# Moving the solve, the joining, the masked product and a Gram between the slots of a delta-rule and gated-MLP kernel

## The chip, the cores and the metric

The kernel runs on one core of one Trainium2 chip. The metric is the device time of one execution in microseconds. The kernel before was timed in three runs: the median is 658.25 us, the runs lie between 656.36 and 658.97 us. The profiled execution is a fourth one; its own time is 657.43 us, and its span, from the first to the last instruction, is 655.6 us.

## The reference

A delta-rule recurrence over 768 tokens for 32 heads of width 48 (4 batches of 8 heads), then a gated MLP on the 3072 rows of width 384:

```python
k_n = k / (norm(k) + 1e-06)
for t in range(768):
    y[t] = q[t] @ state
    state = state + beta[t] * outer(k_n[t], v[t] - k_n[t] @ state)
x = y.transpose(0, 2, 1, 3).reshape(3072, 384)
out = (1 / (1 + exp(-(x @ w_gate))) * (x @ w_val)) @ w_out      # 384 -> 1536 -> 384
```

## The kernel before

The tokens are cut into 12 groups of 64 per head, numbered 0 to 11. For each group the 32 heads' recurrence inside the group is solved in closed form, and the group's 256 rows of the MLP follow.

The recurrence of a group g goes through these functions:

- `gram(g)` (L291): 64 small products of K with itself into two PSUM tiles `pg`; then ten copies to SBUF, six into `G` (L303) and four into `L` (L308), on ACT for every group but the first.
- `norms(g)` (L240 to L273): 18 DVE steps that give the norms `m`, `mq` and the factors `gam`.
- `scale_v(g)` (L279): sixteen ACT instructions that scale V in `kv` by `mq`, in place.
- `solve_halves(g)` for groups 0 to 2 (from group 3 on another routine, `solve`, does the work): 40 steps. The first 4 (L382, L385) prepare `H` and `gs`, the next 30 (L391, L394) are the forward substitution, 2 (L397) copy to `X`. Steps 37 to 40 are what is called the joining here: step 37 transposes `X` to `mt` on DVE (L400) and issues the products `pz` (L407, 64 pairs of 32x32 blocks, listed as x128); step 38 transposes `mt` on DVE (L420) and copies `pz` to `scratch` on ACT (L421); step 39 issues the products `pm`; step 40 subtracts `pm` from `mt` (L428, DVE).
- `masked(g)` (L319): the products `pp` of K and Q, then four DVE multiplications by the mask `pmask` (L324) into `kqp`.
- `rest(g)` (L444, L455): products `pk` of K and the state, and R = V - pk on DVE. `updates(g, 0..2)` (L475, L467) use `mt` and R; `rows(g)` (L501, L504) gives Y in `yy`, copied to `ys` (L508, L510); `flip` (L540, L543) transposes it to `xx`, the MLP's input; `advance(g)` (L522) moves the state on.

The MLP's weights come as 36 pieces of 384 KB (`raw`). `scaled(n)` is a pair of ACT instructions on a piece (L189, L191) and also issues the load of piece n + 6; `join(n)` (L203, DVE) makes the words `u` of it; for the groups from 1 on each piece is split further by `weight_hi` (L212, ACT) and `weight_lo` (L219, DVE) into `w`.

The MLP runs in slots. Slot 2f of group 0 issues the products `gv` of the gate and the value for column tile f (L556; L559 from group 1 on), the odd slots the products `po` of the output for the tile two before (L584; L590). Group g's first slot is 24 g. The element-wise work of a tile is the sigmoid on ACT (L564, `sg`) and the product with the value on DVE (L565). What else goes into a slot stands in tables: `plan[s]` is called behind the slot's products, `late[s]` behind its sigmoid, `tail[s]` at the end. Group 1's recurrence runs in the slots of group 0, group 2's in those of groups 0 and 1.

The order in which the code calls is the order of the instructions on each engine, since the schedule is written out by hand for all engines and each engine takes its instructions in that order. The loads are all issued by SP, in code order too: a load that waits holds up those behind it. Buffers are few: `gv` has two PSUM tiles, `aux` (used by `pg`, `pp`, `pz`, `pm`, `pu`, `yy`, `pt`) two, `row` (used by R and by the output rows `ot`) three, `kqp` two and `X`, `G`, `mt` one.

What stands ahead of slot 0 is written out in full: loads, group 0's recurrence up to its `flip`, and pieces of group 1's. `busy_array` there issues products whose result nobody reads. `W` is 24, `plan`'s entries of group 1's solve are in this line, which gives a slot and a number of steps:

```python
    for at, n in ((0, 12), (1, 4), (2, 4), (3, 4), (5, 1), (6, 1), (7, 1), (8, 1)):
        plan[at].append(steps(halves1, n))
```

Of the kernel before, what the change touches and what calls it, by code (L numbers as in the profile page):

```python
# [55 lines left out]
def deltanet_gated_mlp(ctx: ExitStack, tc: tile.TileContext, kd, qd, kv, beta, words, out):  # L56
# [106 lines left out]
    pieces = [(0, "g"), (0, "v")]  # L163
# [112 lines left out]
    def scale_v(g):  # L276
        V, mq = state[g]["kv"][:, 1], state[g]["mq"]
        for c in range(CP):
            nc.scalar.activation(V[:, c], V[:, c], AF.Copy, scale=mq[:, c, 0:1])  # L279
            yield  # L280

    def gram(g):

        kq, st = kqp[g % 2], state[g]
        st["G"] = G = wk.tile([128, 32, CP], F32, name=f"G_{g}", tag="G", bufs=1)
        st["L"] = L = wk.tile([128, CP, 32], F32, name=f"L_{g}", tag="L", bufs=2)
        pg = [ps_aux.tile([128, J, C], F32, name=f"pg_{g}_{e}", tag="aux") for e in range(2)]
        for j in range(J):
            for e, x in KINDS:
                r, t = 64 * e, tokens_at(e, x)  # L290
                nc.tensor.matmul(out=pg[e][t:t + 64, j], lhsT=kq[r:r + D, x, j], rhs=kq[r:r + D, x, j], start=True, stop=True)  # L291
        return blocks_of(pg, G, L, g == 0)
# [332 lines left out]
    def take(gen, n=1):  # L625
        for _ in range(n):
            next(gen, None)
# [32 lines left out]
        pass  # L660
    second_half(half)
    lower_left(0)
    take(scale_v(0), CP)
    take(gram(1), 10)
    halves0, norms1, halves1 = solve_halves(0), norms(1), solve_halves(1)
    for n in range(2, 4):
        scaled(n)
    take(halves0, 38)
    for n in range(4, 8):
        scaled(n)  # L670
    take(norms1, 11)
    take(halves0, 2)
# [5 lines left out]
    busy_array(gap[0], 5)  # L678
    stage(12, 14, lower_left(1))
    load_rows(1, 0)  # L680
    for n in range(8, 10):
        scaled(n)
    take(masks0, 2)
    updates(0, 1)
# [1 line left out]
    take(norms1, NORMS)  # L686
    updates(0, 2)
    busy_array(gap[0], 5)
    for n in range(10, 12):
        scaled(n)  # L690
    take(joins, 2)
    take(halves1, 12)
    rows(0)
    busy_array(gap[0], 2)
    scaled(12)
    take(joins, 2)
    flip(0, 0)
    flip(0, 1)
    busy_array(gap[0], 2)
    tail = collections.defaultdict(list)  # L700
    for n in range(13, len(pieces)):
        plan[(n - 13) * 4 // 5].append(lambda n=n: scaled(n))
    plan[2].append(lambda: load_k(2))
    spread(joins, len(pieces) - 4, 0, 20)
    for at, n in ((0, 12), (1, 4), (2, 4), (3, 4), (5, 1), (6, 1), (7, 1), (8, 1)):
        plan[at].append(steps(halves1, n))
    spread(splits, 12, 7, 24, into=tail)
    spread(splits, len(pieces) + 1 - 12, 24, 44, into=tail)
    for s in (4, 5):
        plan[s].append(steps(scalings[1], 8))  # L710
    for part in (1, 0):
        plan[8].append(lambda part=part: load_rows(2, part))
    plan[10].append(lambda: load_q(2))
    halves2 = solve_halves(2)
    plan[11].append(lambda: clear(2))
    plan[23].append(lambda: joint(2))
    plan[24].append(lambda: lower_left(2))

# [19 lines left out]
    for g in range(N):  # L738
        w = W * (g - 1)
        if g == 0:  # L740
            late[3].append(lambda: advance(0))
            continue
        up, at_rows = (13, 19) if g < 3 else (10, 16)
        late[w + 10 if g == 1 else w + 6].append(lambda g=g: rest(g))
        for step in range(3):
            late[w + up + 2 * step].append(lambda g=g, step=step: updates(g, step))
        late[w + at_rows].append(lambda g=g: rows(g))
        late[w + at_rows].append(lambda g=g: advance(g))
        for c in range(2):
# [93 lines left out]
```

## Time and profile before

| | |
|---|---|
| time of the profiled execution, its span | 657.43 us, 655.6 us |
| median of three runs | 658.25 us (656.36 to 658.97) |
| PE busy | 626.6 us, 96% of the span |
| PE weight loads busy | 585.8 us, 89% |
| DVE, ACT, POOL busy | 467.9 us (71%), 320.9 us (49%), 11.3 us (2%) |
| mean granted TensorE clock | 0.985 |
| the chain that ended last | PE 90%, DVE 4%, ACT 3%, issue 1%, DMA 1% |

The profile's timeline gives, for an engine, the start and the length of an instruction (or of a run of alike ones, x their number), the line, what is written from what, and in brackets the idle time before it with the engine and line that ended it. The lengths of PE's products overlap by some 0.1 us with the next one's start. The windows give the busy time of each engine in a stretch of the span, and the granted clock of TensorE as a share of full speed.

### The profile page before, as it was taken

The numbers are of one execution on the slowest core, as the hardware profiler recorded it, in microseconds if no ns is written. First come the engines' busy times: TensorE is split into PE (matmuls) and PEld (weight loads), VectorE is DVE, ScalarE is ACT, GpSimd is POOL, SyncE is SP. The second block draws the span as 40 slices with busy tenths as digits, with TensorE's granted clock in tenths as the row PEclk, the third lists the DMA queues.
The fourth block names the chain that finished last, engine by engine and source line by source line (L and its number), as shares of the span: only waits on it lengthen the run. The fifth ranks groups of instructions, "written<-read, shape, count | busy, mean of one in ns | idle before, by whom it ended". The sixth has DMA issues, their size and how long they took to land.

```text
span 655.6 us, 24068 instructions
## 1 busy us (share of the span) xinstructions
PE 626.6 (96%) x10548; PEld 585.8 (89%) x10556; DVE 467.9 (71%) x1443; ACT 320.9 (49%) x870; POOL 11.3 (2%) x30
## 2 busy tenths in 40 slices
PE   6776999899999999999999999999999999999996
PEld 4454778798999999999999999999999999999996
DVE  5886398668887877877977967977977977952221
ACT  4957586455554454454454454454354354333321
POOL 5000000000000000000000000000000000000000
PEclk9988899899999999999999999999999999999999
DMA  9586553110222021122012012013012100000101
GB/s 263 184 272 194 166 138 83 26 27 2 83 51 60 26 51 52 38 48 62 29 44 72 23 41 77 22 39 81 21 33 82 23 8 3 19 9 2 25 1 25
DMA packets 17769, 41.07 MB, mean 63 GB/s; under 512 B 4224, under 2 KB 7296, under 8 KB 17664
## 3 DMA queue, kind: packets, MB, share of 16 engines
q1 hardware_dynamic: 17664, 39.53, 21.1%
q8 instruction: 83, 1.36, 0.9%
q14 instruction: 22, 0.18, 0.1%
HBM read 34.80 MB, written 4.72 MB: 60 GB/s over the span
## 4 chain that ended last, share of the span: by engine, by line
PE 90%; DVE 4%; ACT 3%; issue 1%; DMA 1%; ACTq 0%; SPq 0%; DVEq 0%
PE gv L559 43%; PE po L590 22%; PE gv L556 5%; PE pu L475 3%; PE po L584 2%; PE pg L291 2%; PE pk L444 2%; PE yy L501 2%; PE yy L504 2%; PE pp L319 2%; PE pk L467 1%; PE pd L522 1%; PE pt L540 1%; ACT kv L279 1%; DVE kqp L324 1%
## 5 line engine op out<-in xcount | busy, mean ns | idle before, releaser
L559 PE MATMUL gv<-xx,w 128*128 128x256 f32 x2376 | 308.2, 284 | 0.0
L559 PEld LDWEIGHTS gv<-xx,w 128*128 128x128 f32 x2376 | 302.2, 191 | 0.7
L590 PE MATMUL po<-w,h 128*128 128x384 f32 x792 | 166.4, 345 | 0.2 <-issue 0.2
L564 ACT ACTIVATE sg<-gv 128x256 f32<-128x256 f32 x144 | 55.2, 384 | 208.3 <-PE gv L559 193.2
L590 PEld LDWEIGHTS po<-w,h 128*128 128x128 f32 x792 | 133.3, 188 | 3.5 <-issue 0.4
L565 DVE TENSOR_TENSOR sg<-sg,gv 128x256 f32<-128x256 f32 x144 | 60.3, 419 | 90.6 <-ACT sg L564 90.2
L570 ACT CAST h<-sg 128x256 fp32r<-128x256 f32 x132 | 53.6, 406 | 53.1 <-DVE sg L565 51.5
L350 DVE TENSOR_TENSOR X<-X,tmp 128x126 f32<-128x126 f32 (+22 forms) x279 | 71.3, 256 | 8.9
L347 DVE TENSOR_TENSOR tmp<-X,gp 128x126 f32<-128x126 f32 (+22 forms) x279 | 70.9, 254 | 7.9
L575 DVE TENSOR_TENSOR h<-sg,h 128x256 fp32r<-128x256 f32 x132 | 55.0, 417 | 28.1 <-ACT h L570 28.0
L481 ACT COPY su<-pu 32x384 f32<-32x384 f32 x92 | 43.3, 470 | 14.3 <-PE pu L475 12.9
L279 ACT ACTIVATE kv<-kv,mq 128x48 f32<-128x48 f32 x192 | 48.1, 330 | 0.0
L529 DVE TENSOR_TENSOR su<-su,pd 48x384 f32<-48x384 f32 x40 | 22.1, 552 | 20.5 <-PE pd L522 20.1
L556 PE MATMUL gv<-xx,u 128*128 128x256 f32 x144 | 36.4, 405 | 0.0
L303 ACT COPY G<-pg 32x256 f32<-32x256 f32 (+1 forms) x69 | 25.3, 367 | 18.6 <-PE pg L291 17.3
L324 DVE TENSOR_TENSOR kqp<-pp,pmask 64x512 f32<-64x512 f32 x48 | 32.3, 687 | 2.1 <-PE pp L319 1.1
L556 PEld LDWEIGHTS gv<-xx,u 128*128 128x128 f32 x144 | 28.3, 203 | 5.5 <-issue 0.8
L455 DVE TENSOR_TENSOR R<-kv,pk 128x384 f32<-128x384 f32 x44 | 22.4, 550 | 2.1 <-PE pk L444 2.1
L212 ACT CAST w<-u 128x384 fp32r<-128x384 f32 x36 | 18.2, 509 | 5.4 <-DVE w L219 4.9
L475 PEld LDWEIGHTS pu<-R,mt 32*32 32x32 f32 x1408 | 16.5, 105 | 4.9 <-issue 1.2
L475 PE MATMUL pu<-R,mt 32*32 32x48 f32 x1408 | 19.4, 202 | 0.9 <-DVE kqp L324 0.9
L219 DVE TENSOR_TENSOR w<-u,w 128x384 fp32r<-128x384 f32 x36 | 19.3, 551 | 1.3 <-ACT w L212 1.3
(104 smaller groups left out, 517.7 us busy)
## 6 DMA issues: line engine op xcount, KB each, us to landing
raw<-in_words_dram SPq DMA_DIRECT2D x36, 384.0 KB, 5.2
kv<-in_kv_dram SPq DMA_DIRECT2D x24, 384.0 KB, 5.4
kqp<-in_qd_dram SPq DMA_DIRECT2D x24, 256.0 KB, 4.1
kqp<-in_kd_dram SPq DMA_DIRECT2D x24, 192.0 KB, 3.6
out_dram<-ot SPq DMA_DIRECT2D x48, 96.0 KB, 2.2
beta<-in_beta_dram SPq DMA_DIRECT2D x12, 16.0 KB, 4.5
```

What stands on the lines that cost most here:

```text
L279: nc.scalar.activation(V[:, c], V[:, c], AF.Copy, scale=mq[:, c, 0:1])
L347: nc.vector.tensor_tensor(out=tmp, in0=X[:, k:16, j:j + 1].to_broadcast([128, n, j]), in1=gp[:, j:j + 1, 0:j].to_broadcast([128, n, j]), o ...
L350: nc.vector.tensor_tensor(out=X[:, k:16, 0:j], in0=X[:, k:16, 0:j], in1=tmp, op=ALU.add)
L475: nc.tensor.matmul(out=pu[0 if g else x][r:r + 32, j], lhsT=mt[r:r + 32, e * J + j], rhs=R[e][r:r + 32, j], start=True, stop=True)
L481: nc.scalar.copy(su[r:r + 32, 3 if x else e], pu[0][r:r + 32])
L556: nc.tensor.matmul(out=pg[:, o], lhsT=parts[w, f][:, k * 128:(k + 1) * 128], rhs=x[0][:, k], start=k == 0, stop=k == KC - 1)
L559: nc.tensor.matmul(out=pg[:, o], lhsT=parts[w, f][:, a, k * 128:(k + 1) * 128], rhs=x[b][:, k], start=(k == 0 and q == 0), stop=(k == KC - ...
L564: nc.scalar.activation(h, st["gv", f][:, 0], AF.Sigmoid)
L565: nc.vector.tensor_tensor(out=h, in0=h, in1=st["gv", f][:, 1], op=ALU.mult)
L570: nc.scalar.copy(hh[:, 0], st["sg", f])
L575: nc.vector.tensor_tensor(out=hh[:, 1], in0=st["sg", f], in1=hh[:, 0].bitcast(F32), op=ALU.subtract)
L590: nc.tensor.matmul(out=po[s], lhsT=hh[:, a, ts], rhs=parts["o", f][:, w], start=(f == 0 and q == 0), stop=(f == NF - 1 and q == 2))
```

## The change

The ordering in front of slot 0 and the tables of the slots are changed; no instruction is added or removed.

- Ahead of slot 0, G's ten copies of group 1 are issued ahead of group 0's scalings of V, four `scaled` follow ACT's copy of `pz` where two stood ahead of it, and 4 steps of group 1's solve stand ahead of Y's copy, not 12. K of group 2 is loaded there, not in slot 2.
- Group 1's solve: slots 0 to 5 instead of 0 to 3. Its joining: steps 37 to 40 in slots 9, 10, 10, 11 instead of 5, 6, 7, 8.
- Group 1's masked product: slot 11 instead of 1. Its scalings of V: slots 7 and 8 instead of 4 and 5. Its `rest`: slot 8 instead of 10.
- Group 2's Gram: behind slot 3 instead of slot 8, its copies in slots 4 to 6; its norms and solve from slot 8 on instead of 12. Its scalings: slots 25 to 28 instead of 21 to 24; its `rest`: slot 28 instead of 30; its joining: slots 29, 30, 30, 31 instead of 27 to 30.
- `scaled`, the splits and group 2's loads are moved by a slot or two.

```diff
     lower_left(0)
+    take(gram(1), 10)
     take(scale_v(0), CP)
-    take(gram(1), 10)
...
-    for n in range(2, 4):
-        scaled(n)
     take(halves0, 38)
-    for n in range(4, 8):
+    for n in range(2, 6):
         scaled(n)
...
     load_rows(1, 0)
+    load_k(2)
-    for n in range(8, 10):
+    for n in range(6, 9):
         scaled(n)
...
     take(joins, 2)
-    take(halves1, 12)
+    take(halves1, 4)
     rows(0)
...
-    for at, n in ((0, 12), (1, 4), (2, 4), (3, 4), (5, 1), (6, 1), (7, 1), (8, 1)):
+    for at, n in ((0, 8), (1, 4), (2, 6), (3, 4), (4, 5), (5, 5), (9, 1), (10, 1), (11, 1)):
         plan[at].append(steps(halves1, n))
-    spread(splits, 12, 7, 24, into=tail)
+    plan[10].append(steps(halves1))
+    spread(splits, 12, 9, 24, into=tail)
...
-    for s in (4, 5):
+    for s in (7, 8):
         plan[s].append(steps(scalings[1], 8))
...
-        late[w + 10 if g == 1 else w + 6].append(lambda g=g: rest(g))
+        at_rest = {1: 8, 2: 28}.get(g, w + 6)
+        late[at_rest].append(lambda g=g: rest(g))
...
-            mask_later(1, 1)
+            mask_later(1, 11)
...
-            gram_later(g, w - 16 if g < 4 else w - 18)
+            gram_later(g, {2: 3, 3: 32}.get(g, w - 18))
...
-            scaling(g, w - 3 if g == 2 else w - 5 if g == 3 else w - 7)
-    spread(chain(norms(2), halves2), NORMS + 36, 12, 26, lambda s: max(0.1, 1.6 - busy[s]))
-    for at in (27, 28, 29, 30):
+            scaling(g, {2: 25, 3: 43}.get(g, w - 7))
+    spread(chain(norms(2), halves2), NORMS + 36, 8, 27, lambda s: max(0.1, 1.6 - busy[s]))
+    for at in (29, 30, 30, 31):
         plan[at].append(steps(halves2))
```

Three places of the order. The first is DVE ahead of slot 0, from the last preparation of group 1's solve to the copy of Y (`ys`); before:

```order
L385 SCALAR_TENSOR_TENSOR gs_728<-gp_471,gam_668 128x256
L391 TENSOR_TENSOR tmp_15_733<-H_727,gs_728 128x30
L394 TENSOR_TENSOR H_727<-H_727,tmp_15_733 128x2x15
L391 TENSOR_TENSOR tmp_14_736<-H_727,gs_728 128x28
L394 TENSOR_TENSOR H_727<-H_727,tmp_14_736 128x2x14
L391 TENSOR_TENSOR tmp_13_739<-H_727,gs_728 128x52
L394 TENSOR_TENSOR H_727<-H_727,tmp_13_739 128x2x2x13
L391 TENSOR_TENSOR tmp_12_742<-H_727,gs_728 128x48
L394 TENSOR_TENSOR H_727<-H_727,tmp_12_742 128x2x2x12
L508 COPY ys_779<-yy_1_746 128x8x48
```

Now:

```order
L382 TENSOR_TENSOR H_725<-dmask,gam_666 128x128
L385 SCALAR_TENSOR_TENSOR gs_726<-gp_467,gam_666 128x256
L508 COPY ys_765<-yy_1_732 128x8x48
L203 SCALAR_TENSOR_TENSOR u_778<-raw_102 128x384
L203 SCALAR_TENSOR_TENSOR u_778<-raw_106 128x384
```

The eight substitution steps now stand behind `xx`, in slot 0.

The second is DVE ahead of group 1's joining (L400), from the element-wise product of one tile earlier on; before (tile 2, slots 4 and 5):

```order
L565 TENSOR_TENSOR sg_2_992<-sg_2_992,gv_2_966 128x256
L203 SCALAR_TENSOR_TENSOR u_1003<-raw_611 128x384
L203 SCALAR_TENSOR_TENSOR u_1003<-raw_613 128x384
L400 STREAM_TRANSPOSE mt<-X_563 128x16x16x2
L203 SCALAR_TENSOR_TENSOR u_1092<-raw_618 128x384
```

Now (tile 4, slots 8 and 9; `gp_1062` is group 2's norms):

```order
L240 STREAM_TRANSPOSE gp_1062<-G_918 128x1024
L565 TENSOR_TENSOR sg_4_1064<-sg_4_1064,gv_4_1040 128x256
L455 TENSOR_TENSOR R_0_1101<-kv_113,pk_0_1067 128x384
L455 TENSOR_TENSOR R_1_1102<-kv_113,pk_1_1068 128x384
L203 SCALAR_TENSOR_TENSOR u_1111<-raw_776 128x384
L203 SCALAR_TENSOR_TENSOR u_1111<-raw_803 128x384
L400 STREAM_TRANSPOSE mt<-X_559 128x16x16x2
```

R's two subtractions now stand between the tile's product and L400; on ACT the sixteen scalings of V still stand close ahead of that tile's sigmoid.

The third is ACT around group 2's joining, from tile 1's sigmoid of group 1 on (`ot` are group 0's last output rows); before:

```order
L564 ACTIVATE sg_1_1874<-gv_1_1852 128x256
L212 CAST w_1878<-u_1092 128x384
L212 CAST w_1881<-u_1092 128x384
L594 COPY ot_0_1885<-po_0_995 128x384
L594 COPY ot_1_1889<-po_1_996 128x384
L570 CAST h_1_1960<-sg_1_1874 128x256
L212 CAST w_1963<-u_1106 128x384
L421 COPY scratch_1755<-pz_1894 128x512
```

Now:

```order
L564 ACTIVATE sg_1_1866<-gv_1_1839 128x256
L212 CAST w_1870<-u_1013 128x384
L212 CAST w_1873<-u_1013 128x384
L594 COPY ot_0_1877<-po_0_983 128x384
L594 COPY ot_1_1881<-po_1_984 128x384
L279 ACTIVATE kv_1015<-kv_1015,mq_1425 128x48 x4
L570 CAST h_1_1889<-sg_1_1866 128x256
L212 CAST w_1892<-u_1030 128x384
L279 ACTIVATE kv_1015<-kv_1015,mq_1425 128x48 x4
L564 ACTIVATE sg_2_1918<-gv_2_1894 128x256
```

Eight of group 2's scalings of V and tile 2's sigmoid now stand ahead of the joining's copy L421. On DVE, group 2's L400 stood behind tile 1's product and two L219; now it stands behind tile 1's product, three L219, L575, tile 2's product, R's two subtractions and one more L219.

More of the change, by code (lines that the diff above doesn't have):

```diff
@@ L688, in deltanet_gated_mlp @@
     busy_array(gap[0], 5)
-    for n in range(10, 12):
+    for n in range(9, 11):
         scaled(n)
     take(joins, 2)
-    take(halves1, 12)
+    take(halves1, 4)
     rows(0)
     busy_array(gap[0], 2)
-    scaled(12)
+    for n in range(11, 13):
+        scaled(n)
     take(joins, 2)
@@ L700, in deltanet_gated_mlp @@
     tail = collections.defaultdict(list)
-    for n in range(13, len(pieces)):
-        plan[(n - 13) * 4 // 5].append(lambda n=n: scaled(n))
-    plan[2].append(lambda: load_k(2))
+    for n, at in enumerate((0, 0, 0, 1, 2, 2, 4, 5, 6, 8, 9, 10, 11, 12, 12, 13, 14, 15, 16, 16, 17, 18, 18), 13):
+        plan[at].append(lambda n=n: scaled(n))
     spread(joins, len(pieces) - 4, 0, 20)
-    for at, n in ((0, 12), (1, 4), (2, 4), (3, 4), (5, 1), (6, 1), (7, 1), (8, 1)):
+    for at, n in ((0, 8), (1, 4), (2, 6), (3, 4), (4, 5), (5, 5), (9, 1), (10, 1), (11, 1)):
         plan[at].append(steps(halves1, n))
-    spread(splits, 12, 7, 24, into=tail)
+    plan[10].append(steps(halves1))
+    spread(splits, 12, 9, 24, into=tail)
     spread(splits, len(pieces) + 1 - 12, 24, 44, into=tail)
-    for s in (4, 5):
+    for s in (7, 8):
         plan[s].append(steps(scalings[1], 8))
     for part in (1, 0):
-        plan[8].append(lambda part=part: load_rows(2, part))
-    plan[10].append(lambda: load_q(2))
+        plan[6].append(lambda part=part: load_rows(2, part))
+    plan[8].append(lambda: load_q(2))
     halves2 = solve_halves(2)
-    plan[11].append(lambda: clear(2))
+    plan[12].append(lambda: clear(2))
     plan[23].append(lambda: joint(2))
@@ L751, in deltanet_gated_mlp @@
             busy[w + at_rows + 2] += 0.6
-        busy[w + 10 if g == 1 else w + 6] += 1.1
+        busy[at_rest] += 1.1
         busy[w + up + 2] += 1.1
```

## The prediction

> **What bounds the kernel now.** I read the page, then PE's list of waits over the first 130 us, then PE's timeline there with the windows of the granted clock beside it. The chain that ended last is nine tenths PE (the table in front), so what counts is where PE waits and where its clock is low.
>
> ```profile
> PE pz L407 <- DVE mt L400: 6.6, 2, 4.5
> ```
>
> Of PE's waits this is the longest: two joinings wait 6.6 us for DVE's transposition L400. On the timeline the first lies inside group 0's slots, the second where group 1's begin:
>
> ```profile
> 42.63 1.51 PE L540 MATMUL pt<-ident,ys 128*128 128x128 f32 x6 [2.32 <-DVE ys L508]
> 44.88 3.25 PE L556 MATMUL gv<-xx,u 128*128 128x256 f32 x12
> 61.41 1.82 PE L407 MATMUL pz<-mt,scratch 32*32 32x32 f32 x119 [4.46 <-DVE mt L400]
> 65.25 0.33 PE L407 MATMUL pz<-mt,scratch 32*32 32x32 f32 x9 [2.03 <-issue]
> 65.51 4.87 PE L556 MATMUL gv<-xx,u 128*128 128x256 f32 x12
> 70.22 1.45 PE L584 MATMUL po<-u,sg 128*128 128x384 f32 x4
> 71.61 1.29 PE L407 MATMUL pm<-scratch 32*32 32x32 f32 x128
> 72.82 2.86 PE L556 MATMUL gv<-xx,u 128*128 128x256 f32 x12
> 75.61 1.16 PE L291 MATMUL pg<-kqp 48*64 48x64 f32 x64
> 80.78 1.15 PE L444 MATMUL pk<-su,kqp 48*64 48x48 f32 x64
> 108.89 0.82 PE L540 MATMUL pt<-ident,ys 128*128 128x128 f32 x6
> 120.31 1.45 PE L584 MATMUL po<-u,sg 128*128 128x384 f32 x4
> 123.95 1.78 PE L407 MATMUL pz<-mt,scratch 32*32 32x32 f32 x128 [2.19 <-DVE mt L400]
> 125.67 3.29 PE L559 MATMUL gv<-xx,w 128*128 128x256 f32 x18
> 128.80 1.22 PE L590 MATMUL po<-w,h 128*128 128x384 f32 x6
> 131.32 2.42 PE L559 MATMUL gv<-xx,w 128*128 128x256 f32 x18
> ```
>
> ```profile
> 59.00:60.00 1.00, 0.00 (x0) 0.00 (x0) 0.72 (x2) 1.00 (x3) 0.00 (x0) 0.69 0.68 252
> 69.00:70.00 1.00, 1.00 (x4) 0.78 (x3) 0.00 (x0) 0.00 (x0) 0.00 (x0) 0.69 0.00 0
> 124.00:125.00 1.00, 1.00 (x91) 1.00 (x95) 1.00 (x3) 0.79 (x3) 0.00 (x0) 0.62 0.16 35
> ```
>
> A wait costs more than its idle time. The third number from the end is the granted clock: it falls in the window from 59 us and rises in the one from 69, and a gv product between takes 4.87 us, not 2.86. Group 1's joining so loses 4.46 idle, 2.03 of "issue" (PE waits for nothing that the profile shows; its own code, I think), 0.9 in pz (1.82 + 0.33 against pm's 1.29) and 2.0 in gv: 9.4 us. Group 2's loses 2.19, then 0.5 in pz and 0.9 in gv (3.29 against 2.42): 3.6 us. Behind the 2.32 us that Y's transposition waited, gv shows 0.4 too much.
>
> **Ahead of slot 0.**
>
> ```profile
> 23.79 2.06 PE L416 MATMUL pz<-mt,wide 64*64 64x32 f32 x64 [0.28 <-DVE mt L400]
> 26.60 0.58 ACT L421 COPY scratch<-pz 128x512 f32<-128x512 f32 x1
> 38.64 1.14 PE L504 MATMUL yy<-su,kqp 128*64 128x48 f32 x32
> 40.05 0.19 DVE L391 TENSOR_TENSOR tmp<-H,gs 128x30 f32<-128x30 f32 x1
> 41.93 0.56 DVE L508 COPY ys<-yy 128x384 f32<-128x384 f32 x1
> ```
>
> Group 0's pz ended at 25.85, ACT copied it at 26.60, behind two pieces. These now come later, and G's copies and V's scalings take the same time in either order, so L421 starts 0.65 earlier, and with it all that hangs on pm. It is worth 0 if something else holds that chain, 0.75 at most; I take 0.6. Y's products ended at 39.78, but DVE went through eight solve steps from 40.05 to 41.93 before it copied Y: 1.9 us gone, with certainty, as the four steps that stay end at 40.05. The transposition then comes right behind the products, so the clock has no reason to fall, and 1.51 becomes 0.82: 0.65. Sum 3.1 (from 1.9 to 3.3), and 0.4 in slot 0's gv.
>
> The eight steps are now in slot 0, where DVE waited for the sigmoid later on; they cost nothing as long as joins and products of slots 0 to 6 keep ahead of PE, and by my count DVE still idles there before tile 3's product. ACT's three pieces of slot 0 must have landed. K of group 2, 384 KB in two loads, now goes ahead of nine pieces on SP's queue and delays their landing by about a microsecond; a piece is used six pieces after it was asked for, some 6 us, so I take 0. POOL's clearing of X and group 2's other loads move by two slots at most, with nobody near to wait for them.
>
> **Group 1's joining.** Its prices:
>
> ```profile
> 20.87 2.31 ACT L303 COPY G<-pg 128x256 f32<-128x256 f32 x6
> 23.20 1.49 ACT L308 COPY L<-pg 32x256 f32<-32x256 f32 x4
> 53.21 1.92 ACT L527 COPY su<-pd 48x384 f32<-48x384 f32 x4
> 56.93 1.91 ACT L279 ACTIVATE kv<-kv,mq 128x48 f32<-128x48 f32 x8
> 58.86 0.38 ACT L564 ACTIVATE sg<-gv 128x256 f32<-128x256 f32 x1
> 60.02 1.90 ACT L279 ACTIVATE kv<-kv,mq 128x48 f32<-128x48 f32 x8
> 60.55 0.71 DVE L400 STREAM_TRANSPOSE mt<-X 128x512 f32<-128x512 f32 x1
> 81.98 1.02 DVE L455 TENSOR_TENSOR R<-kv,pk 128x384 f32<-128x384 f32 x2 [0.26 <-PE pk L444]
> ```
>
> Before, L400 came late since tile 2's product waited for a sigmoid that stood behind eight scalings (56.93, then 58.86). The new order repeats it at tile 4. I count from the end of the state's product pd in slot 3. PE (overlaps of 0.1 taken off): pg 1.1, three gv of 2.7, two po of 1.4, to the end of tile 4's gv 12.0; then pk 1.1 and po 1.4, so it is ready for pz at 14.5. ACT from the same point: the state's copies 1.9, four pieces of 0.9 (58.86 to 60.02 is a sigmoid of 0.3 and a piece), G's copies 2.3, L's 1.5, two sigmoids 0.6, sixteen scalings 3.8: 13.7, so tile 4's sigmoid, whose gv was done at 12.0, ends at 14.1. DVE then: the product 0.35, R 0.95, two joins 0.95, L400 0.7: 17.0. PE starts pz 0.1 later and has idled 2.6 us (the ends: none, and the 4.46 of before); all of PE's work stands behind pz, so this counts in full. Half clock after that: pz and gv lost 1.4 behind an idle time of 2.19, so I take 1.2, since 2.6 us needn't fall into one window. New loss 3.8 instead of 9.4.
>
> [...]
>
> The new neighbours: pd and pg, 128 small products, now follow each other, where code could come late; between 0 and the 2.03 shown, I take 0.4, as 64 alone showed none at 75.61. The masked product at slot 11 needs pm's buffer, freed by L428. DVE reaches the end of L428 (priced as L400) some 2.4 us after tile 5's gv, PE comes there after pm and po, 2.6 us: nothing, but without spare. Its four masks, 2.7 us on DVE, then lie beside gv of slot 12, before updates in slot 13 that want the buffer. Group 1's `rest` is off the path: mt is needed in slot 13 only.
>
> **Group 2's joining.**
>
> ```profile
> 112.62 1.00 ACT L279 ACTIVATE kv<-kv,mq 128x48 f32<-128x48 f32 x4
> 119.95 1.38 DVE L324 TENSOR_TENSOR kqp<-pp,pmask 64x512 f32<-64x512 f32 x2
> 122.81 0.51 ACT L212 CAST w<-u 128x384 fp32r<-128x384 f32 x1 [1.51 <-DVE w L219]
> 123.22 0.85 ACT L594 COPY ot<-po 128x384 f32<-128x384 f32 x2
> ```
>
> It moves back by one tile, so PE has a gv (2.3), pk (1.1) and a po (1.1) more: on the times of before it would be ready at 121.76 + 4.5 = 126.25, not 121.76 (120.31 + 1.45). But the masks keep DVE busy until 121.33 as before, X's second copy follows them, and the cast that waited until 122.81 waits until 123.0. Behind it ACT has now: casts 0.8, `ot` 0.75, h 0.3, eight scalings 2.0, tile 2's sigmoid 0.4: 127.25. DVE: product 0.35, R 0.95, a split 0.5, L400 0.7, so pz starts at 129.85: idle 3.6 us instead of 2.2 (ends 2.2 and 4.5). With 1.4 for the clock as before this joining loses 5.0, not 3.6: 1.4 worse.
>
> **Sum**, against the profiled execution: -3.1 - 0.4 - 5.6 (9.4 to 3.8) + 0.4 + 1.4 = -7.3, so 657.43 becomes 650.1. The median of the runs shown is 0.8 higher; for runs I say 650.5.
>
> **The rivals.**
> - Group 1's joining is covered after all. For it: ACT's chain has twenty terms, and some copies may run beside gaps that I didn't see; against it: tile 4's sigmoid would have to come 1.5 us sooner and the rest shrink too. It takes away the 3.8: 646.7.
> - Group 1's joining again stops for code (2.03) and pays a second half-clock window (1.7, half of the 3.3 us that the fall at 124 lasted): +3.7, 654.2; with all of before's loss 656. For it: both stood behind each other before. Against: no other pz stopped for code.
> - Y comes no earlier, since something other than the solve steps holds the transposition: +3.1, 653.6. Only the end of yy at 39.78 could, and it allows the gain.
> - Slower: K's load waits for Y's products, as they read the same tile, and holds up the pieces behind it on SP.
>
> ```profile
> 35.26 15.49 SPq L172 DMA_DIRECT2D raw<-in_words_dram  x9
> 86.76 0.84 SPq L105 DMA_DIRECT2D kqp<-in_kd_dram  x2
> 103.69 1.35 SPq L109 DMA_DIRECT2D kqp<-in_qd_dram  x2
> ```
>
> These nine pieces would then start near 40 us, not at 35.26; ACT, which ends ahead of the first joining without idle time, passes each late microsecond on, with half of one more for the clock: 5 us late cost 7.5, and from there on the change loses: 658 to 660. Against it: group 3's K was loaded at 86.76, long before Y's products of group 1, for which its Q waited until 103.69. So K waits for its own readers only.
>
> **How the numbers follow.** 0.5% (3.3 us) is about what a measurement of this kernel can tell from no change, so faster means under 655.0. Forecast 0.55 (648 to 653), covered joining 0.17, code and clock again 0.15 (two thirds of it above 655), no gain at Y 0.08, slower 0.05. Faster: 0.55 + 0.17 + 0.08 and a little of the third; slower 0.05 with its tail; the rest is the same. The range leaves out the slower case, half of the case with code and a part of the covered one: 646 to 656.
>
> **What would show it.** Right: Y's transposition near 40.1 without a wait, slot 0 near 41.8; group 1's pz behind po of slot 9 with 2 to 3 us idle, the sigmoid before it late behind L279; group 2's pz idle 3 to 4 us, longer than before; the rest of the trace alike, shifted. Wrong: idle before pz of group 1 under 1 us or over 4, PE waiting for L428 at the masked product, ACT waiting for pieces in slots 0 to 4, or a stop of PE for code at pd and pg.

## The result and the profile after

The changed kernel took 651.71 us (median of five runs, 650.23 to 653.05), the kernel before 656.36 us in five runs on the same chip (655.90 to 658.97). The ratio is 0.9915, with a 95% interval from 0.9887 to 0.9944: 4.65 us faster, 1.2 us above the 650.5 us that were predicted. The profiled execution took 652.21 us, its span is 650.5 us (before 657.43 and 655.6), and the mean granted clock 0.991 (before 0.985). Of the kernels run later, two executions lie far off and are left out of the figures below: one of 2078.95 us, with the filling products, and one of 687.92 us at a granted clock of 0.844, with the early transpositions and the old slots.

PE's timeline of the changed kernel, at the same places as before: ahead of slot 0, the two joinings, and the updates of groups 1 and 2 (the columns: start, length, engine, line, operation, number, and the idle time ahead with what ended it):

```profile
30.91 0.28 PE L475 MATMUL pu<-kv,mt 32*32 32x48 f32 x5 [1.04 <-issue]
36.83 0.37 PE L475 MATMUL pu<-kv,mt 32*32 32x48 f32 x14 [1.22 <-issue]
41.29 0.84 PE L540 MATMUL pt<-ident,ys 128*128 128x128 f32 x6 [0.44 <-ACT raw L191]
42.88 5.42 PE L556 MATMUL gv<-xx,u 128*128 128x256 f32 x24 [0.31 <-DVE xx L543]
48.22 0.94 PE L522 MATMUL pd<-su,kv 64*48 64x48 f32 x64
48.98 1.13 PE L291 MATMUL pg<-kqp 48*64 48x64 f32 x64
66.53 1.93 PE L407 MATMUL pz<-mt,scratch 32*32 32x32 f32 x128 [3.31 <-DVE n L244]
68.39 5.00 PE L556 MATMUL gv<-xx,u 128*128 128x256 f32 x12
76.02 1.16 PE L319 MATMUL pp<-kqp 48*64 48x64 f32 x64
81.19 0.88 PE L475 MATMUL pu<-R,mt 32*32 32x48 f32 x64
123.58 1.75 PE L407 MATMUL pz<-mt,scratch 32*32 32x32 f32 x128 [3.36 <-DVE mt L400]
125.26 3.34 PE L559 MATMUL gv<-xx,w 128*128 128x256 f32 x18
144.43 0.88 PE L475 MATMUL pu<-R,mt 32*32 32x48 f32 x64 [0.88 <-DVE kqp L324]
```

The same two updates in the kernel before:

```profile
87.23 0.88 PE L475 MATMUL pu<-R,mt 32*32 32x48 f32 x64
149.44 0.88 PE L475 MATMUL pu<-R,mt 32*32 32x48 f32 x64 [0.88 <-DVE kqp L324]
```

Y's transposition waits 0.44 us, not 2.32 (for `ys`, which DVE wrote until 41.14 us), and slot 0 starts at 42.88 us, 2.0 earlier than before. Group 1's joining waits 3.31 us, without the stop of 2.03 us. The name in the bracket, L244, is the instruction that happened to end last by the profile; what pz reads is `mt`, which L400 wrote from 65.68 to 66.39 us. Group 2's joining waits longer than before, 3.36 us against 2.19. Group 1's first update in slot 13 (the pu at 81.19) stood at 87.23 us before, group 2's (144.43) at 149.44: of the 6.04 us won up to the one, 5.01 are left at the other, and 5.1 at the end of the span.

ACT and DVE ahead of group 1's joining:

```profile
58.58 1.90 ACT L279 ACTIVATE kv<-kv,mq 128x48 f32<-128x48 f32 x8
61.28 1.90 ACT L279 ACTIVATE kv<-kv,mq 128x48 f32<-128x48 f32 x8
63.08 0.36 ACT L564 ACTIVATE sg<-gv 128x256 f32<-128x256 f32 x1
60.46 1.24 DVE L240 STREAM_TRANSPOSE gp<-G 128x1024 f32<-128x1024 f32 x1
63.48 0.42 DVE L565 TENSOR_TENSOR sg<-sg,gv 128x256 f32<-128x256 f32 x1 [1.78 <-ACT sg L564]
65.68 0.71 DVE L400 STREAM_TRANSPOSE mt<-X 128x512 f32<-128x512 f32 x1
```

The chain is the one foretold: tile 4's sigmoid ends at 63.44 us behind sixteen scalings, and DVE's product, R, two joins and L400 stand behind it.

Windows of one microsecond of the changed kernel (behind the stretch: its length, then the busy share and instructions of PE, PE's loads, DVE, ACT and POOL, the granted clock, the DMA share, GB/s):

```profile
65.00:66.00 1.00, 0.00 (x0) 0.00 (x0) 1.00 (x3) 0.63 (x2) 0.00 (x0) 0.96 1.07 208
72.00:73.00 1.00, 1.00 (x4) 0.83 (x3) 0.00 (x0) 0.00 (x0) 0.00 (x0) 0.62 0.08 16
123.00:124.00 1.00, 0.42 (x48) 0.46 (x52) 1.00 (x3) 0.10 (x1) 0.00 (x0) 0.98 0.12 21
127.00:128.00 1.00, 1.00 (x9) 1.00 (x9) 0.00 (x0) 0.00 (x0) 0.00 (x0) 0.82 0.00 0
```

Between the rows at 65 and 72, and between those at 123 and 127, the clock is 0.50. So behind two waits of nearly the same length it stayed at half for different times: some 6.8 us from the end of the window at 65 to inside that at 72, and 3.4 us from the end of that at 123 to inside that at 127.

The moments themselves show more. With 1.00 up to the change and 0.50 behind it, a share of 0.96 at 65 puts the fall at 65.92 us, 0.62 at 72 the rise at 72.76, and 0.98 and 0.82 put the second pair at 123.96 and 127.36. Group 1's pz started at 66.53 us, 0.61 behind the fall, and the clock stayed down for 6.8 us; group 2's had started at 123.58, ahead of the fall, and it was 3.4 us. Worked out in the same way from windows of one microsecond of this trace and of those of before and of three kernels below (us):

| kernel | wait | idle | PE back at | clock falls at | time at half clock |
|---|---|---|---|---|---|
| before | Y's transposition | 2.32 | 42.63 | 42.32 | 3.4 |
| before | group 1's joining | 4.46, then the stop of 2.03 inside pz | 61.41 | 59.38 | 10.2 |
| before | group 2's joining | 2.19 | 123.95 | 124.24 | 3.4 |
| changed | group 1's joining | 3.31 | 66.53 | 65.92 | 6.8 |
| changed | group 2's joining | 3.36 | 123.58 | 123.96 | 3.4 |
| four solve steps alone | group 1's joining | 4.95 | 58.77 | 59.06 | 3.4 |
| group 2's joining back | group 1's joining | 5.11 | 67.36 | 65.66 | 6.8 |
| group 2's joining back | group 2's joining | 2.19 | 118.19 | 120.26 | 3.4 |
| masked product moved | group 1's joining | 1.91 | 55.91 | 56.54 | 3.4 |

4.95 us of idle time were followed by 3.4 us at half clock, 3.31 us by 6.8. So the length of a wait alone doesn't set its price.

### The profile page after: what moved, and what is told of

It reads as the page before. It is cut to its first block, busy times and chain, and to the rows that moved or that the text cites. A ratio compares the mean times of both kernels' runs of the same rounds, so it can differ in the third digit from the quotient of the medians.

```text
span 650.5 us, 24072 instructions
## 1 busy us (share of the span) xinstructions
PE 626.4 (96%) x10556; PEld 585.0 (90%) x10556; DVE 467.9 (72%) x1443; ACT 321.2 (49%) x870; POOL 11.3 (2%) x30
## 3 DMA queue, kind: packets, MB, share of 16 engines
q8 instruction: 83, 1.36, 0.9%
## 4 chain that ended last, share of the span: by engine, by line
PE 89%; DVE 5%; ACT 3%; issue 1%; DMA 1%; ACTq 0%; SPq 0%; DVEq 0%
PE gv L559 43%; PE po L590 22%; PE gv L556 4%; PE pu L475 3%; PE pg L291 2%; PE yy L501 2%; PE yy L504 2%; PE pp L319 2%; PE po L584 2%; PE pd L522 2%; PE pk L444 1%; PE pk L467 1%; PE pt L540 1%; ACT kv L279 1%; DVE kqp L324 1%
## 5 line engine op out<-in xcount | busy, mean ns | idle before, releaser
L575 DVE TENSOR_TENSOR h<-sg,h 128x256 fp32r<-128x256 f32 x132 | 55.1, 417 | 29.8 <-ACT h L570 29.8
L556 PE MATMUL gv<-xx,u 128*128 128x256 f32 x144 | 35.8, 402 | 0.3 <-DVE xx L543 0.3
L556 PEld LDWEIGHTS gv<-xx,u 128*128 128x128 f32 x144 | 28.2, 201 | 5.5 <-ACT xx L543 0.8
L475 PEld LDWEIGHTS pu<-R,mt 32*32 32x32 f32 x1408 | 16.5, 105 | 4.9 <-issue 1.7
L219 DVE TENSOR_TENSOR w<-u,w 128x384 fp32r<-128x384 f32 x36 | 19.4, 550 | 1.5 <-ACT w L212 1.4
L475 PE MATMUL pu<-R,mt 32*32 32x48 f32 x1408 | 19.4, 202 | 0.9 <-DVE kqp L324 0.9
```

The lines of the kernel that those rows point to most:

```text
L475: nc.tensor.matmul(out=pu[0 if g else x][r:r + 32, j], lhsT=mt[r:r + 32, e * J + j], rhs=R[e][r:r + 32, j], start=True, stop=True)
L556: nc.tensor.matmul(out=pg[:, o], lhsT=parts[w, f][:, k * 128:(k + 1) * 128], rhs=x[0][:, k], start=k == 0, stop=k == KC - 1)
L575: nc.vector.tensor_tensor(out=hh[:, 1], in0=st["sg", f], in1=hh[:, 0].bitcast(F32), op=ALU.subtract)
```

## The experiments

Eleven kernels were timed in four groups, each in five rounds against the kernel before (medians of before: 656.99, 655.61, 656.08 and 656.07 us). The traces are one execution of each kernel. Ratios are to the kernel before. In the kernels with early transpositions four or five lines are added, so that L400 reads L401, L407 L411, L475 L480, L556 L561 and so on; in the one with filling products two, so that L556 reads L558.

**Which part brings the gain? Four solve steps ahead of Y, alone** (the kernel before, and nothing else of the change):

```diff
-    take(halves1, 12)
+    take(halves1, 4)
...
-    for at, n in ((0, 12), (1, 4), (2, 4), (3, 4), (5, 1), (6, 1), (7, 1), (8, 1)):
+    for at, n in ((0, 20), (1, 4), (2, 4), (3, 4), (5, 1), (6, 1), (7, 1), (8, 1)):
```

> The kernel before with one part of the change: 4 solve steps ahead of Y's copy, the other 8 in slot 0, all else as before. Theory (the steps held Y's copy, and PE's idle time behind it brought the clock down): the transposition starts 1.9 us sooner, takes 0.8 us, not 1.5, gv of slot 0 is 0.4 shorter: slot 0 starts 2.5 us sooner; group 1's joining stays as late against slot 0 as it was or up to 1 us worse, so 1.5 to 3 us less than before. Rival (the gain is given back at the joining, as DVE has 1.9 us more to do ahead of it): the wait at group 1's joining grows from 4.5 to 6.4 us, time as before.

652.48 us (651.26 to 657.39), ratio 0.9939 (0.9912 to 0.9967): the interval overlaps that of the whole change. PE's timeline of this kernel:

```profile
42.16 2.83 PE L556 MATMUL gv<-xx,u 128*128 128x256 f32 x12 [0.31 <-DVE xx L543]
58.77 1.78 PE L407 MATMUL pz<-mt,scratch 32*32 32x32 f32 x128 [4.95 <-DVE mt L400]
81.14 0.88 PE L475 MATMUL pu<-R,mt 32*32 32x48 f32 x64
```

Slot 0 starts 2.7 us earlier than before, about the 1.9 + 0.65 that I had put on Y. Group 1's joining still waits 4.95 us, but the stop of 2.03 us inside it is gone, although nothing was moved there on PE. The first update in slot 13 starts at 81.14 us, and in the changed kernel at 81.19: up to there the four steps alone win as much in these traces as the whole change, with the joining in its old slots.

**G's copies ahead of V's scalings, alone** (the kernel before, with `gram(1)`'s ten copies first and the pieces ahead of slot 0 nearly as in the change):

```diff
     lower_left(0)
+    take(gram(1), 10)
     take(scale_v(0), CP)
-    take(gram(1), 10)
...
-    for n in range(2, 4):
-        scaled(n)
     take(halves0, 38)
-    for n in range(4, 8):
+    for n in range(2, 6):
         scaled(n)
...
-    for n in range(8, 10):
+    for n in range(6, 9):
         scaled(n)
...
-    for n in range(10, 12):
+    for n in range(9, 12):
         scaled(n)
```

> The kernel before with G's copies ahead of V's scalings alone (and its pieces in the order that this gives); Y still behind twelve solve steps, everything else in its old slot. L421 starts 0.7 us earlier. In the kernels run so far PE's stop at the first small products of pu ended at 30.6 to 31.6 us in whichever order ACT works, though PE reached them 0.4 to 0.7 us earlier with G's copies first. If that stop takes the gain, slot 0 starts at 44.5 to 45.2 us (44.88 before) and the time is within 1 us of the kernel before. If the 0.6 us that I predicted come through, slot 0 starts at 44.2 to 44.3, and the time is 1 us lower or more, since the first joining follows.

657.97 us (654.20 to 660.59), ratio 1.0024 (0.9996 to 1.0051): no gain. PE ahead of slot 0, with both of PE's stops, and in group 1's joining:

```profile
30.85 0.28 PE L475 MATMUL pu<-kv,mt 32*32 32x48 f32 x5 [1.31 <-issue]
37.05 0.37 PE L475 MATMUL pu<-kv,mt 32*32 32x48 f32 x14 [1.49 <-issue]
45.63 4.73 PE L556 MATMUL gv<-xx,u 128*128 128x256 f32 x12
67.16 0.33 PE L407 MATMUL pz<-mt,scratch 32*32 32x32 f32 x9 [1.73 <-issue]
```

The last five products of pu's first burst start at 30.85 us; in the kernel before, with a stop of 0.75 us ahead of them, they did at 30.92. PE gets there 0.6 us earlier and stops nearly that much longer. Slot 0 is 0.75 us later than before, since the second stop is longer too (1.49 us, not 0.67).

The stop inside group 1's pz is here again, 1.73 us ahead of the same nine products. So the two traces with twelve solve steps ahead of Y have it, and none of the eleven with four does. That speaks against an accident of one execution; what ties it to those kernels isn't shown.

**Are those stops due to transfers that share the DMA engines?** Two pieces and Q of group 1 are asked for later:

```diff
-    stage(10, 12, state[0]["joint"])
-    load_q(1, state[0]["joint"])
...
-    stage(12, 14, lower_left(1))
+    held = lower_left(1)
+    stage(10, 12, held)
+    load_q(1, held)
+    stage(12, 14, held)
```

> The changed kernel with two weight pieces and Q of group 1 (four transfers, 1.28 MB) asked for some 6 us later, at the copy of group 1's lower left block (32.2 us) and not at the joint's copy (25.9 us). If PE's stop of 1.04 us at 30.9 us, with no wait that the profile shows, comes from code that has to share the DMA engines with these transfers, it falls under 0.4 and slot 0 starts at 41.5 to 42; the time is 650.5 to 651. If the stop has nothing to do with them, it stays at 0.7 to 1.6 us and the time at 651.5 to 652; if the late words are then missed by ACT in slots 0 to 4, group 1's joining idles 4 to 5 us, and the time is 653 to 654.

655.15 us (653.50 to 656.49), ratio 0.9977 (0.9953 to 1.0002): the change's gain is gone. Rows of PE, ACT and PE:

```profile
30.95 0.28 PE L475 MATMUL pu<-kv,mt 32*32 32x48 f32 x5 [1.31 <-issue]
46.62 0.55 ACT L189 ACTIVATE raw<-raw 128x384 int32<-128x384 uint16 x1 [2.88 <-DMA raw<-in_words_dram]
69.70 1.93 PE L407 MATMUL pz<-mt,scratch 32*32 32x32 f32 x128 [6.45 <-DVE n L244]
```

The stop stays, so these transfers don't make it: SP issues them from 32.98 us on here, when the stop is over; in the changed kernel it issues Q at 29.87 us, and the DMA share is 0.76 in the window at 30. The run shows instead what late words cost: ACT waits for a piece at 46.62 us, in the first slots, and group 1's joining, whose chain begins on ACT, passes that on: 6.45 us idle, not 3.31. I had expected 4 to 5.

**What does the slow clock cost at group 1's joining?** Fourteen products whose result nobody reads fill PE's wait:

```diff
+        if g == 1:
+            busy_array(pz, 14)
         if g:
             blocks(pz, A, mt)
```

> The changed kernel with 14 idle-filling products (into pz's own buffer, read by nobody) ahead of group 1's pz, so that PE is busy for about 3.0 of the 3.3 us in which it waited. Theory (the clock falls because PE idles, and the slow clock costs 2.9 us behind the wait): pz takes 1.3 us and the gv product behind it 2.8, not 1.9 and 5.0; pz still starts 3.3 us behind po, so 2.5 to 2.9 us less than the changed kernel, about 649. Rival (gv is slow behind the joining for another reason, such as DVE's or ACT's traffic in PSUM): gv stays at 5 us and the time at 651 to 653.

653.33 us (650.82 to 657.15), ratio 0.9949 (0.9925 to 0.9974): no better than the change. PE there:

```profile
61.87 3.18 PE L99 MATMUL pz<-dmask 128*128 128x512 bf16 x14
65.37 1.29 PE L407 MATMUL pz<-mt,scratch 32*32 32x32 f32 x128 [0.31 <-DVE mt L400]
66.58 2.64 PE L558 MATMUL gv<-xx,u 128*128 128x256 f32 x11
73.18 0.22 PE L407 MATMUL pm<-scratch 32*32 32x32 f32 x2 [1.86 <-issue]
```

pz now takes 1.29 us and not 1.93, and gv runs at full speed, with the granted clock at 1.00 in all windows from 63 to 71 us: the 2.8 us of pz and gv were the clock's. But PE stops for 0.40 us within gv and for 1.86 in pm, and behind the second stop the clock falls after all, by the length of the po at 73.32 us: 2.93 us, not 1.5. So the gain is used up. That the slow clock follows from PE's idle time is shown, with 0.31 us idle ahead of pz here and 3.31 in the changed kernel; the time isn't won.

**What holds L400? V's scalings two slots later:**

```diff
-    for s in (7, 8):
+    for s in (9, 10):
         plan[s].append(steps(scalings[1], 8))
...
-        at_rest = {1: 8, 2: 28}.get(g, w + 6)
+        at_rest = {1: 10, 2: 28}.get(g, w + 6)
```

> The changed kernel with V's sixteen scalings of group 1 two slots later (slots 9 and 10, the group's rest of that work with them). My theory of group 1's joining: tile 4's sigmoid ends late on ACT, since sixteen scalings and two pieces stand ahead of it, and DVE's L400 stands behind the product of that sigmoid; without them the sigmoid comes 3.8 us sooner, so the idle 3.3 us goes to under 1, with it the slow clock of 2.9 us: 646 to 647. Rival, something else than the scalings sets L400 (the copies of G and L, joins on DVE): idle stays 2.5 to 3.3 us and the time 651 to 652. Second rival, the scalings then delay a later sigmoid ahead of group 1's updates: half of the gain, 648 to 650.

651.69 us (650.52 to 652.65), ratio 0.9904 (0.9877 to 0.9931). My expectation fell. ACT, DVE and PE:

```profile
59.81 0.38 ACT L564 ACTIVATE sg<-gv 128x256 f32<-128x256 f32 x1 [0.29 <-PE gv L556]
60.39 1.24 DVE L240 STREAM_TRANSPOSE gp<-G 128x1024 f32<-128x1024 f32 x1
62.21 0.41 DVE L565 TENSOR_TENSOR sg<-sg,gv 128x256 f32<-128x256 f32 x1
64.33 1.44 PE L407 MATMUL pz<-mt,scratch 32*32 32x32 f32 x128 [3.27 <-DVE nt L251]
```

The sigmoid is done at 60.19 us, but DVE takes up its product at 62.21: group 2's L240 and three small steps of its norms, which the change moved to slot 8, stand ahead. From the end of pd the product now starts after 13.9 us (62.21 less 48.28); with the scalings in place it was 14.3 (63.48 less 49.16). ACT's chain hid a second one on DVE that ends 0.4 us sooner. R left the stretch too (0.95 us), and PE's pk with it (1.1), so the idle time stayed.

**Both chains out of the way** (that kernel, and group 2's norms from slot 10):

```diff
-    spread(chain(norms(2), halves2), NORMS + 36, 8, 27, lambda s: max(0.1, 1.6 - busy[s]))
+    spread(chain(norms(2), halves2), NORMS + 36, 10, 27, lambda s: max(0.1, 1.6 - busy[s]))
```

> The changed kernel with V's scalings of group 1 in slots 9 and 10 (which alone left 3.27 us idle ahead of group 1's joining and 651.7 us, although tile 4's sigmoid then ended at 60.2 us) and with the norms of group 2 from slot 10, not 8. If the joining's wait had two chains of nearly the same end, ACT's scalings and then DVE's own L240 (1.24 us) with three small steps behind three joins, tile 4's product starts near 60.5 us, not 62.2, L400 1.7 us sooner, and the idle time falls to 1.3 to 1.8 us with at most one half-clock window: 647.5 to 650. If something third holds DVE, the idle time stays at 3 us and the time at 651 to 652.

651.08 us (648.71 to 652.26), ratio 0.9916 (0.9884 to 0.9948). PE's timeline:

```profile
31.05 0.28 PE L475 MATMUL pu<-kv,mt 32*32 32x48 f32 x5 [1.58 <-issue]
63.50 1.28 PE L407 MATMUL pz<-mt,scratch 32*32 32x32 f32 x128 [1.36 <-DVE mt L400]
69.74 0.65 PE L407 MATMUL pm<-scratch 32*32 32x32 f32 x52 [1.39 <-issue]
74.18 1.26 PE L319 MATMUL pp<-kqp 48*64 48x64 f32 x62 [0.96 <-issue]
```

The idle time fell to 1.36 us, as the two chains ask, and the clock stayed at full speed behind it (1.00 in all windows from 60 to 73 us). So the joining loses 1.4 us instead of 6.1. The time still missed the expectation. The stops of 1.39 and 0.96 us behind the joining took half of that back, and at group 2's joining PE idled 3.4 us as in the changed kernel. The stop of 1.58 us ahead of slot 0 brought the clock down, by the length of the pk at 33.28 us behind it: 1.50 us, against 0.99 behind a stop of the same length at the same place in the kernel that follows. The mean granted clock of the execution is 0.992 all the same, against 0.991 in the changed kernel's, so it was low elsewhere for nearly as long.

**The transposition ahead of the product, group 1.** X is complete long before: L397 ends at 56.5 us in the changed kernel. The two transpositions are issued as soon as it is, in slot 6:

```diff
+EARLY = (1,)
...
         nc.vector.transpose(mt.rearrange("q c (k r) -> q k c r", r=2), X.rearrange("q k (c r) -> q k c r", r=2))
+        if g in EARLY:
+            nc.vector.transpose(D.rearrange("q c t -> q (c t)"), mt.rearrange("q c t -> q (c t)"))
+            yield
...
-        nc.vector.transpose(D.rearrange("q c t -> q (c t)"), mt.rearrange("q c t -> q (c t)"))
+        if g not in EARLY:
+            nc.vector.transpose(D.rearrange("q c t -> q (c t)"), mt.rearrange("q c t -> q (c t)"))
...
-    for at, n in ((0, 8), (1, 4), (2, 6), (3, 4), (4, 5), (5, 5), (9, 1), (10, 1), (11, 1)):
+    for at, n in ((0, 8), (1, 4), (2, 6), (3, 4), (4, 5), (5, 5), (6, 1), (9, 1), (10, 1), (11, 1)):
```

> The changed kernel with group 1's two transpositions of the joining (L400, L420) issued in slot 6, right behind X; pz and pm stay in slots 9 and 10. Theory (L400 is late only because it stands on DVE behind tile 4's product, R and two joins, and these behind a sigmoid that ACT's scalings hold up): no wait ahead of pz, no slow clock, the whole 6.3 us gone, 0 to 1.3 of it given back at pm, whose copy of pz waits on ACT: 645.5 to 647. Rival (the joining would wait for something else, X's substitution or code): pz still waits 1 us or more, 649 to 651.

648.04 us (646.67 to 648.58), ratio 0.9860 (0.9827 to 0.9892):

```profile
63.88 1.29 PE L411 MATMUL pz<-mt,scratch 32*32 32x32 f32 x128
65.10 2.86 PE L561 MATMUL gv<-xx,u 128*128 128x256 f32 x12
```

No wait at group 1's joining, and no slow clock by the lengths of pz and gv: 1.29 and 2.86 us, 1.93 and 5.00 in the changed kernel. This is the case that the prediction had as a rival, at 646.7 us: the joining covered. Here the edit brings it about.

**Group 2's joining, back in its old slots** (the changed kernel with group 2's scalings in slots 21 to 24, its `rest` in slot 30, its joining in 27 to 30):

```diff
-        at_rest = {1: 8, 2: 28}.get(g, w + 6)
+        at_rest = {1: 8}.get(g, w + 6)
...
-            scaling(g, {2: 25, 3: 43}.get(g, w - 7))
+            scaling(g, {2: 21, 3: 43}.get(g, w - 7))
-    spread(chain(norms(2), halves2), NORMS + 36, 8, 27, lambda s: max(0.1, 1.6 - busy[s]))
+    spread(chain(norms(2), halves2), NORMS + 36, 8, 26, lambda s: max(0.1, 1.6 - busy[s]))
-    for at in (29, 30, 30, 31):
+    for at in (27, 28, 29, 30):
```

> The changed kernel with group 2's scalings, rest and joining in the slots of before (21 to 24, 30, 27 to 30). Theory (the later joining is the worse one: its wait grew from 2.2 to 3.4 us through eight scalings ahead of tile 2's sigmoid): the wait is 2.2 us again, 1.0 to 1.4 us less than the changed kernel, about 650.5. Rival (the change is right for group 2, and the wait of before would be longer now since less DVE work lies ahead of it in shorter time): the wait is over 3.4 us, 652 or more.

651.62 us (649.16 to 653.06), ratio 0.9911 (0.9879 to 0.9943). ACT in the first slots, then PE at both joinings:

```profile
45.10 0.56 ACT L189 ACTIVATE raw<-raw 128x384 int32<-128x384 uint16 x1 [2.64 <-DMA raw<-in_words_dram]
67.36 1.93 PE L407 MATMUL pz<-mt,scratch 32*32 32x32 f32 x128 [5.11 <-DVE n L244]
118.19 1.59 PE L407 MATMUL pz<-mt,scratch 32*32 32x32 f32 x128 [2.19 <-DVE mt L400]
```

Group 2's wait is 2.19 us again, so the change did cost the 1.2 us of idle time there. The median shows no gain, and the profile says where it can go: this execution reached slot 0 at 41.91 us, 1.0 earlier than the changed kernel's, ACT then waited 2.64 us for words, and group 1's joining idled 5.11 us.

**Both joinings early** (the changed kernel with group 2's transpositions in slot 27 as well):

```diff
-EARLY = (1,)
+EARLY = (1, 2)
...
-    for at in (29, 30, 30, 31):
+    for at in (27, 29, 30, 30, 31):
```

> The changed kernel with mt's and D's transpositions (L400 and L420) of groups 1 and 2 issued by DVE as soon as X is complete (slots 6 and 27), ahead of the tile's product. If each joining of the changed kernel waits only because L400 stands behind that product on DVE, group 2's 3.4 us idle and its 1.4 us of slow clock go as well, on top of the 648.0 us with group 1's transposition early: 643 to 644.5. If PE's stops for code take the place of the waits, as 0.9 us did behind group 1's joining, 645 to 646. If group 2's joining waits for something beside L400 (R, a copy on ACT), 647 to 648.

643.30 us (642.48 to 645.20), ratio 0.9780 (0.9754 to 0.9807). Neither pz waits:

```profile
62.83 1.39 PE L411 MATMUL pz<-mt,scratch 32*32 32x32 f32 x128
115.62 1.33 PE L411 MATMUL pz<-mt,scratch 32*32 32x32 f32 x128
```

The second joining was worth 4.7 us beyond the first (648.04 less 643.30, in different groups of runs; by the trace of the change 3.36 idle and 1.4 of clock). It is the fastest of all the kernels run, by 8.4 us against the changed one, again between groups.

**Do the later slots matter, then?** The early transpositions on the kernel with the four steps alone, joinings and all else in the old slots:

```diff
+EARLY = (1, 2)
...
-    for at, n in ((0, 20), (1, 4), (2, 4), (3, 4), (5, 1), (6, 1), (7, 1), (8, 1)):
+    for at, n in ((0, 20), (1, 4), (2, 4), (3, 4), (4, 1), (5, 1), (6, 1), (7, 1), (8, 1)):
...
-    for at in (27, 28, 29, 30):
+    for at in (26, 27, 28, 29, 30):
```

> The kernel before with four solve steps ahead of Y, and with the same early transpositions (slots 4 and 26); everything else of the change left out: G's copies behind V's scalings, joinings, scalings, Gram and masked product in their old slots. That kernel without early transpositions gave 652.5 us with 4.95 us idle ahead of group 1's joining and 2.19 ahead of group 2's, and some 1.5 and 1.0 us of slow clock behind them. If the transposition's place is all that a joining waits for, 652.5 - 6.4 - 3.2 = 643, no slower than the changed kernel with the same (643 to 644.5), and the later slots of the change buy nothing. If the later slots are needed to give DVE and ACT time ahead of the joinings, idle time stays at group 1's joining: 646 to 648.

650.03 us (649.49 to 652.49), ratio 0.9887 (0.9853 to 0.9921), 6.7 us behind the one before. DVE and PE:

```profile
49.61 2.70 DVE L325 TENSOR_TENSOR kqp<-pp,pmask 64x512 f32<-64x512 f32 x4
57.57 1.93 PE L411 MATMUL pz<-mt,scratch 32*32 32x32 f32 x128 [3.68 <-DVE mt L401]
```

The first expectation (643) fell, and the bound of 646 to 648 for the other was too low. From slot 0 to that joining DVE has hardly a gap: 32 solve steps and copies, joins, and four masks of 2.7 us. So one more part was moved alone.

**The masked product in slot 11, on that kernel:**

```diff
-            mask_later(1, 1)
+            mask_later(1, 11)
```

> The kernel before with four solve steps ahead of Y and the early transpositions (which gave 650.0 us, 3.68 us idle ahead of group 1's joining), and with one more part of the change: the masked product of group 1 in slot 11, not 1. If DVE is simply full between slot 0 and that joining, with four masks of 2.7 us in all among its work, L401 comes 2.7 us sooner; PE comes 1.1 us sooner too, as the product pp no longer stands ahead: idle 3.68 - 2.7 + 1.1 = 2.1 us, one half-clock window at most behind it, 646.5 to 648.5. If the joining waits there for something else than DVE's amount of work (a sigmoid on ACT, words that land late), the idle time stays at 3.5 to 4.8 us and the time at 650 to 651.

646.68 us (646.22 to 654.85), ratio 0.9871 (0.9826 to 0.9916):

```profile
55.91 1.61 PE L411 MATMUL pz<-mt,scratch 32*32 32x32 f32 x128 [1.91 <-DVE mt L401]
57.45 4.08 PE L561 MATMUL gv<-xx,u 128*128 128x256 f32 x12
123.83 0.26 PE L411 MATMUL pm<-scratch 32*32 32x32 f32 x7 [1.65 <-issue]
```

The idle time came down to 1.91 us (expected 2.1): the amount of work on DVE held that joining. The median is 3.4 us lower, but in another group of runs, and the intervals of the two ratios overlap. The profiled execution itself is one of the long ones (651.09 us), with stops of 1.48 and 1.22 us ahead of slot 0 and of 1.65 in group 2's pm.

## Why the prediction was right, and where not

The time fell into the range and on the predicted side; the sum was 2.2 us too good. That the time came within 1.2 us of the forecast is in part luck: the forecast started from a median of 658.25 us, and the kernel before took 656.36 in the five runs beside the result, so 4.65 us were won where 7.75 had been forecast. By its own terms, on the profiled executions:

| step | predicted | measured | from |
|---|---|---|---|
| ahead of slot 0 | -3.1 | -2.0 | slot 0 at 42.88, was 44.88 |
| gv of slot 0 at full clock | -0.4 | -0.4 | two gv in 5.42 |
| code at pd and pg | +0.4 | 0 | 48.22 and 48.98, no stop |
| group 1's joining | -5.6 | -3.3 | 9.4 to 3.31 + 0.64 + 2.14 = 6.1 |
| small seams from slot 0 to slot 13 | 0 | -0.3 | the rest of 6.04 |
| group 2's joining | +1.4 | +1.0 | 62.21 us between the two pu rows, then 63.24 |
| all that follows | 0 | -0.1 | the span's end |
| sum | -7.3 | -5.1 | 655.6 to 650.5 |

- **Y, right.** The eight steps and the transposition's speed gave what was counted; the four steps alone gave it as well (2.7 us), and most of the gain of the whole change with it (652.48 us against 656.99, each a median).
- **L421, mis-sized.** It starts at 25.88 us, 0.72 earlier, as said, and the prediction named the case that it is worth 0 "if something else holds that chain". Something does: PE's stop in pu's first burst, which ended at 30.91 us against 30.92. The second stop took half a microsecond more, 1.22 us where it had been 0.67. G's copies first, alone, showed no gain.
- **Group 1's joining, right in its chain, mis-sized in the clock and in what the moving wins.** Twenty terms gave ACT 13.7 us to tile 4's late sigmoid; it was 63.08 less 49.16, 13.9. The idle time was 3.31 us for 2.6, since PE came 0.4 sooner and DVE 0.3 later. The clock was the real miss: 0.64 in pz and 2.14 in gv (5.00 us long, 2.14 above its full-speed time to the next start) are 2.8 us, not 1.2. I had reckoned with a little less than the 1.4 us behind group 2's joining of before, where the clock was at half for 3.4 us, and here it was 6.8. That 2.6 us "needn't fall into one window", the ground for 1.2 and not 1.4, no run shows; what the runs showed is 3.4 us at half clock behind a wait of 3.36 us and 6.8 behind one of 3.31. And 2.03 of the 9.4 us that I counted for the old place were the stop inside pz, which is gone as well where only the solve steps were moved. There the joining in its old place lost 6.4 us (4.95 idle, 0.49 in pz and 0.97 in gv), and from slot 0 to the first update in slot 13 it took 38.98 us; the changed kernel took 38.31. So by these traces the moving itself won some 0.7 us, where 5.6 had been put on it; the rest of the 3.3 came with the solve steps. The reason given, sixteen scalings, was only the first of two: without them DVE's own chain held L400 nearly as long.
- **Group 2's joining, right.** 3.36 us idle for 3.6, clock 1.4 for 1.4; undone, the 2.19 came back.
- **Masked product, pd and pg, right.** The first starts without a wait at 76.02 us; no stop stands at pd and pg.
- **K's load, doubtful.** It was put at 0. The microsecond by which it was to delay the pieces was my estimate; 384 KB at the 369 and 357 GB/s of the windows at 40 and 41 us of before are 1.1 us. ACT waited 0.17 us for words in the profiled execution, and the prediction had named such a wait as a sign of being wrong. With the change's order of loads, ACT also waited for words in the first slots in the kernels with the filling products (0.53 and 0.32 us), with both chains out of the way (1.45) and with group 2's joining back (2.64); with the old order it did not in the kernel before and in the one with early transpositions and the old slots. No run moves K's load alone, so its part isn't shown.
- **The rivals.** A second stop at that pz did not come, but the longer half clock of that rival did (6.8 us). That joining 1 is covered came true only when the transposition was moved for it.

What stays open: what makes PE stop where the profile shows no wait. The stops differ from trace to trace, up to 2.03 us, and by the runs above neither Q's and the pieces' transfers nor what stands ahead of them on ACT decides their end. That it is PE's own code arriving fits their place, nearly always among many small products (the 0.40 us within gv is an exception), but no run shows it.

## What to carry to other kernels

Where a product waits for a short instruction that stands behind a tile's regular work on its engine, issue that instruction when its input is complete, rather than moving the whole step: 8.4 us came from issuing the transpositions of two joinings early, while the moving alone had only exchanged one such place for another. The early issue needs the time that the later slots give DVE: with the old slots it took 650.03 us, not 643.30. Price a wait on PE by its idle time and by the time at half clock behind it, here 3.4 to 10.2 us, and look for the second chain that ends just ahead of the one that you see. An instant won ahead of a stop or of a load at its limit is not yet won: check what comes next in that chain.

## What the runs showed of the hardware

- A wait of PE of 1.36 us left the granted clock at 1.00; waits of 1.91, 3.31 and 3.36 us brought it to 0.50, for about 3.4, 6.8 and 3.4 us. Length alone doesn't decide: 4.95 us with the four steps alone were followed by 3.4 us at half clock. 2.19 us at group 2's joining brought the clock down for 3.4 us in the kernel before and in the one with that joining back; with the four steps alone it did not for as long, since the mean clock of 0.997 over the span of 649.7 us is worth 3.9 us at half clock in all (3.2 to 4.5 by its last digit), and 3.4 of them lie behind group 1's joining. A stop of 1.58 us brought it down in one trace and not in two others, by the length of the pk behind it (1.50 us, and 0.99 in the two).
- Half clock cost 1.4 us at group 2's joining and 2.8 at group 1's in the changed kernel, behind idle times of 3.36 and 3.31 us. Group 2's pz started 0.38 us ahead of the fall, group 1's 0.61 behind it.
- PE's stops without a visible wait, up to 2.03 us, come nearly all in bursts of 64 or 128 small products, and differ between kernels of nearly the same code: 2.03, 1.73 and none at the same pz; 0.75 to 1.58 at the same five products of pu, with nearly the same end (30.6 to 31.7 us).
- In the two traces where ACT waited 2.64 and 2.88 us for a 384 KB piece in the first slots, group 1's joining idled 1.8 and 3.1 us longer (5.11 and 6.45 us against 3.31).
